# A gated attention and a two-layer net in one hand-ordered program: unit 3's k and q turned by transfers, tiles shared by pairs of units, another order of work

## The chip, the core and the metric

The kernel runs on one core of a Trainium2 chip. A core has five engines that run side by side, each through its own instructions in order: TensorE (PE, matrix products and transposes into the eight PSUM banks), VectorE (DVE), ScalarE (ACT), GpSimd (POOL) and SyncE (SP, which issues the transfers here). Transfers run on 16 DMA engines. An instruction that needs another engine's result waits on a semaphore, and everything behind it on its engine waits too. The metric is the device time of one execution in microseconds (us), lower is better; the median over runs is taken.

## What is computed

```python
def _attn_ref(q, k, v, f_logit):
    f = 1.0 / (1.0 + np.exp(-f_logit))
    state = np.zeros((B, H, D, D))
    for t in range(S):
        state = f[:, :, t, :, None] * state + np.einsum('bhd,bhe->bhde', k[:, :, t], v[:, :, t])
        y[:, :, t] = np.einsum('bhd,bhde->bhe', q[:, :, t], state)

def _moe_ref(x, w_in, w_out):
    h = x @ w_in
    g = np.maximum(0.01 * h, h)
    return g @ w_out

def reference(...):
    x = attn_out.transpose(0, 2, 1, 3).reshape(B * S, H * D)
    return _moe_ref(x, w_in, w_out)
```

B, H, S, D are 4, 8, 768, 48: 4 batches, 8 heads, 768 steps, 48 values a head. So x is 3072 x 384, w_in 384 x 2048 and w_out 2048 x 384. Inputs and output are float32; the kernel multiplies in bfloat16 and adds in float32.

## The kernel before

**Units.** The 768 steps are cut into 6 chunks of 128. The work is staged in 12 units of 256 rows of x. Units 0 to 3 hold one batch each, chunks 0 and 1 ("paired": neighbouring steps share a row of the tile, and a unit's halves are its heads 0 to 3 and 4 to 7). Units 4 to 11 hold two batches each at one chunk from 2 to 5, and their halves are the batches. A state goes on from chunk to chunk, so a unit needs the units of the same batches before it.

**Steps of a unit.** The gates' logits are loaded, and ScalarE makes the softplus of their negative (ge, line 236, and gl, 248). TensorE adds these up over the steps (cs, 257 to 268), ScalarE takes the exponentials (dec, 276 to 285: em for k, at for q, end for the state). VectorE or GpSimd scales k and q by them (line 301). k and q have to be turned, so that the head's values lie along the partitions. That is done in one of two ways: by TensorE (tk, tq: four transposes a half, line 335) with a copy out of PSUM by VectorE or ScalarE (ck, cq, 348 and 350), or by a DMA transpose of the whole unit that SP issues (xk, xq, 355). TensorE multiplies the turned k and q (sc, 371 and 378), VectorE masks the result (mk, 388 and 392), TensorE adds masked scores times v and q times state (mx and ms, 409), and ScalarE or VectorE copies x, already transposed, into the x tile (xt, 469 and 471). The state is updated by pt (482, 487), sf (497, 499) and sb (505, 508).

**The two layers.** A first-layer word (up, 516) is six matmuls of 128 x 256 into one bank; ScalarE applies the leaky relu on the way out (pr, 521) into the g tile. A second-layer word (dn, 528) is four matmuls of 128 x 384. The last half tile goes in two column halves (dh, 550; oh, 557 and 559; sh). ob (572, 574) copies the result into an osb tile and st (578) stores it. Weights are loaded by WI and WO in float32 into staging tiles (`parts_in`, two of 384 KB, and `ring`, three of 768 KB) and cast to bfloat16 by cw (199, 201).

**Fillers.** id_N (207) is N groups of 128 columns of matmul over a tile of ones, whose result nobody reads, four groups to an instruction.

**Order.** One string, `order`, lists all words, some 800 of them, and each word's function is called in that order. Each engine's instructions, and the transfers on SP's queue, come in just this order; nothing reorders them. A word such as `up_2_5@5` is first-layer group 5 of unit 2 into bank 5; a last number of a copy or scaling chooses the engine. The framework adds the waits by which tiles an instruction reads and writes.

**What the change touches.** `lasts` (line 69) and `osbs` (79) have memory of their own. There are three x tiles (77) and three g tiles (78), one unit in each, chosen by `xTs[j % 3]` and `gTs[j % 3]`. Units 0 to 3 turn k and q by TensorE, units 4 to 11 by DMA transposes.

Of the kernel before, what the change touches and what calls it, by code (L numbers as in the profile page):

```python
# [15 lines left out]
def kernel(  # L16
# [442 lines left out]
    def x_out(j, i, e):  # L459
        src = banks[st[j].pop(("py", i))][:, 0:KD]  # L460
        xT = xTs[j % 3]
        if paired(j):
            src = src.rearrange("t (k s n) -> t k s n", k=NK, s=2)
            dst = xT[:, :, i, :].rearrange("t k (n s) -> t k s n", s=2)
        else:
            src = src.rearrange("t (k n) -> t k n", k=NK)
            dst = xT[:, :, i, :]
        if e:
            nc.scalar.copy(out=dst, in_=src)  # L469
        else:  # L470
            nc.vector.tensor_copy(out=dst, in_=src)  # L471
# [37 lines left out]

    def up(j, g, bank):  # L510
        st[j]["pm", g] = bank
        pm = banks[bank].rearrange("t (i n) -> t i n", i=2)
        for i in range(2):
            ff = 2 * g + i
            for kk in range(NK):
                nc.tensor.matmul(pm[:, i, :], w_in_of(ff, kk), xTs[j % 3][:, kk].rearrange("t a s -> t (a s)"),  # L516
                                 start=(kk == 0), stop=(kk == NK - 1))
# [4 lines left out]

    def down(j, a, quarter, *bank):
# [3 lines left out]
        for ff in range(4 * quarter, 4 * quarter + 4):  # L527
            nc.tensor.matmul(po, gTs[j % 3][:, ff, 128 * a:128 * a + 128], w_out_b[quarter][:, ff % 4, :],  # L528
# [164 lines left out]
```

## Time and profile before

| | us |
|---|---|
| median of 3 runs (177.96 to 178.77) | 178.56 |
| the profiled execution | 178.35 |
| its span, from the first to the last recorded event | 176.6 |
| TensorE busy in it | 170.0 |
| ScalarE, VectorE, GpSimd busy | 119.7, 89.3, 55.9 |

The profile page lists each engine's busy time, then the span in 40 slices of 4.4 us (a digit is the busy share of a slice in tenths, PEclk the clock granted to TensorE, DMA the busy share of the transfer engines). A group row names line, engine, operation, out<-in and count, then the busy time, the mean length of one in ns, and the idle time just before, with what ended it. A row in order of time begins with its start and length. An instruction's length includes the time until its result is there; matmuls follow each other closer than that, so their cost is read from start to start.

### The profile page before, as it was taken

The numbers are of one execution on the slowest core, as the hardware profiler recorded it, in microseconds if no ns is written. First come the engines' busy times: TensorE is split into PE (matmuls) and PEld (weight loads), VectorE is DVE, ScalarE is ACT, GpSimd is POOL, SyncE is SP. The second block draws the span as 40 slices with busy tenths as digits, with TensorE's granted clock in tenths as the row PEclk, the third lists the DMA queues.
The fourth block names the chain that finished last, engine by engine and source line by source line (L and its number), as shares of the span: only waits on it lengthen the run. The fifth ranks groups of instructions, "written<-read, shape, count | busy, mean of one in ns | idle before, by whom it ended". The sixth has DMA issues, their size and how long they took to land.

```text
span 176.6 us, 5545 instructions
## 1 busy us (share of the span) xinstructions
PE 170.0 (96%) x2295; PEld 129.7 (73%) x2295; DVE 89.3 (51%) x194; ACT 119.7 (68%) x244; POOL 55.9 (32%) x103
## 2 busy tenths in 40 slices
PE   7998989999899999999999999999999999999992
...
PEclk9999999999999999999999999999999999999999
DMA  5999999999899888789899899999889993300023
GB/s 139 282 301 262 344 341 339 388 296 219 185 198 193 166 182 162 171 214 206 169 203 207 213 182 183 189 242 205 190 170 208 196 222 112 137 4 0 0 71 111
DMA packets 106856, 34.44 MB, mean 195 GB/s; under 512 B 101072, under 2 KB 105040, under 8 KB 106832
## 3 DMA queue, kind: packets, MB, share of 16 engines
...
q8 instruction: 18, 0.29, 0.7%
...
## 4 chain that ended last, share of the span: by engine, by line
PE 71%; SPq 14%; DMA 10%; POOL 1%; issue 1%; DVE 1%; ACT 0%; DVEq 0%
PE ps L516 30%; PE ps L528 29%; SPq L158 9%; PE ps L409 5%; DMA ring<-in_moe_w_in_dram 4%; DMA k_raw<-in_k_dram 3%; DMA ring<-in_moe_w_out_dram 3%; SPq L162 3%; SPq L176 3%; PE ps L378 3%; PE ps L550 2%; PE ps L265 1%; PE ps L487 1%; POOL w_out L201 1%; ACT w_in L199 0%
## 5 line engine op out<-in xcount | busy, mean ns | idle before, releaser
L516 PE MATMUL ps<-xT,w_in 128*128 128x256 bf16 x576 | 70.0, 273 | 0.7 <-ACT w_in L199 0.7
L521 ACT ACTIVATE gT<-ps 128x512 bf16<-128x512 f32 x96 | 55.6, 610 | 21.6 <-PE ps L516 19.3
L528 PE MATMUL ps<-w_out,gT 128*128 128x384 bf16 x368 | 68.4, 326 | 0.0
L516 PEld LDWEIGHTS <-w_in 128*128 128x128 bf16 x576 | 60.8, 110 | 6.2 <-ACT w_in L199 0.9
L528 PEld LDWEIGHTS <-gT 128*128 128x128 bf16 x368 | 34.2, 98 | 19.1
L392 DVE TENSOR_TENSOR wm<-ps,ut 128x512 bf16<-128x512 f32 x32 | 20.1, 684 | 14.0 <-ACT gT L521 8.0
L307 POOL CAST vb<-v_raw 128x768 bf16<-128x768 f32 (+1 forms) x11 | 8.1, 738 | 31.7 <-DMA v_raw<-in_v_dram 29.1
L505 POOL TENSOR_TENSOR sf<-sf,end 128x192 f32<-128x192 f32 x12 | 6.9, 571 | 31.3 <-DVE sf L499 27.5
L301 POOL TENSOR_TENSOR kh<-k_raw,em 128x768 bf16<-128x768 f32 (+1 forms) x8 | 11.7, 1458 | 12.8 <-DMA k_raw<-in_k_dram 6.7
L301 DVE TENSOR_TENSOR qh<-q_raw,at 128x384 bf16<-128x384 f32 (+1 forms) x11 | 9.2, 845 | 11.4 <-DMA q_raw<-in_q_dram 7.8
L574 DVE COPY osb<-ps 128x384 f32<-128x384 f32 x12 | 6.6, 556 | 15.0 <-PE ps L528 13.5
L276 ACT ACTIVATE em<-ps 128x384 bf16<-128x384 f32 x24 | 12.1, 503 | 2.0 <-PE ps L265 1.2
L469 ACT CAST xT<-ps 128x384 bf16<-128x384 f32 x11 | 5.6, 534 | 11.1 <-PE ps L409 11.0
L236 ACT ACTIVATE f_raw<-f_raw 128x384 f32<-128x384 f32 (+1 forms) x16 | 10.8, 689 | 3.1 <-DMA f_raw<-in_f_logit_dram 2.9
L508 POOL CAST sb<-sf 64x192 bf16<-64x192 f32 x30 | 11.3, 376 | 3.6 <-DVE sf L497 1.9
L471 DVE CAST xT<-ps 128x384 bf16<-128x384 f32 x13 | 7.2, 567 | 10.1 <-PE ps L409 10.0
L277 ACT ACTIVATE at<-ps 128x384 bf16<-128x384 f32 x24 | 12.2, 508 | 0.0
L499 DVE TENSOR_TENSOR sf<-sf,ps 64x192 f32<-64x192 f32 x32 | 11.2, 351 | 0.7
L207 PE MATMUL ps<-warm 128*128 128x512 bf16 (+3 forms) x31 | 10.2, 441 | 1.1 <-DVE warm L83 1.1
L388 DVE TENSOR_TENSOR wm<-ps,pair_mask 128x512 bf16<-128x512 f32 x16 | 10.1, 686 | 1.9 <-PE ps L371 1.8
L248 ACT ACTIVATE lf<-f_raw 128x384 bf16<-128x384 f32 (+1 forms) x16 | 10.7, 687 | 0.2
L572 ACT COPY osb<-ps 128x384 f32<-128x384 f32 x11 | 5.3, 479 | 8.1 <-PE ps L528 8.0
...
## 6 DMA issues: line engine op xcount, KB each, us to landing
...
```

Source lines behind the costliest of these rows:

```text
L158: nc.sync.dma_start(out=by_pair(raw(j, x))[:, h].rearrange("t h s d -> t h (s d)"), in_=srcs[x][j, h, 0:2 * C, :].rearrange("h (t s) d -> ...
L236: nc.scalar.activation(gates(j)[:, part], gates(j)[:, part], AF.Exp, scale=-1.0)
L248: nc.scalar.activation(dst, src, AF.Ln, bias=1.0)
L276: nc.scalar.activation(ems[j % 2][:, a], t[:, 0:H * D], AF.Exp, scale=1.0)
L277: nc.scalar.activation(ats[j % 2][:, a], t[:, 0:H * D], AF.Exp, scale=-1.0)
L301: eng.tensor_mul(heads(j, to[j % NR], a)[:, :, :, 0:D], raw_heads(j, x, a), decays(j, by, a))
L392: nc.vector.tensor_mul(w, src.rearrange("t (p n) -> t p n", p=P2), ut[:, None, :].to_broadcast([128, P2, 128]))
L499: nc.vector.tensor_add(sf[rows], sf[rows], new)
L508: eng.tensor_copy(out=sb[rows, :, y * D:y * D + D], in_=sf[rows])
L516: nc.tensor.matmul(pm[:, i, :], w_in_of(ff, kk), xTs[j % 3][:, kk].rearrange("t a s -> t (a s)"), start=(kk == 0), stop=(kk == NK - 1))
L521: nc.scalar.activation(gTs[j % 3][:, 2 * g:2 * g + 2, :], pm, AF.Prelu, alpha=0.01)
L528: nc.tensor.matmul(po, gTs[j % 3][:, ff, 128 * a:128 * a + 128], w_out_b[quarter][:, ff % 4, :], start=(ff == 0), stop=(ff == NF - 1))
```

## The change

It has four parts. x and g tiles hold a pair of units each and there are two of either, so that four units' strips exist where three did; `x_of` and `g_of` pick a unit's strip. `osbs` and `lasts` become views of the staging tiles. Two functions, `up_both` and `relu_both` with the words uq and pq, are added that would do one first-layer product for both units of a pair. The order is new throughout: 785 words instead of 795. In it, unit 3's tk, tq, ck and cq (8 words) are replaced by xk_3 and xq_3; the fillers are 30, 33, 7, 5, 17, 19, 5 and 3 groups instead of 40, 16, 4, 3, 3, 5, 3, 16, 5, 6, 8 and 3; the engines of some copies and scalings are others. TensorE has 2282 matmuls instead of 2295. No word uq or pq stands in the new order. The diff, with the order cut to its start, the stretch around units 2 to 5, and its end:

```diff
@@ -66,7 +66,6 @@
     ems = tiles(2, [128, 2, H * D], BF16, "em")
     ats = tiles(2, [128, 2, H * D], BF16, "at")
     ends = tiles(4, [128, 2, P2], FP32, "end")
-    lasts = tiles(2, [128, 2 * H * D], FP32, "last")
     vbs = tiles(3, [128, 2, H, D], BF16, "vb")
     v2s = tiles(3, [128, 2 * P2, 4, 16], BF16, "v2")
     kTs = tiles(2, [128, 2 * P2, 128], BF16, "kT")
@@ -74,9 +73,8 @@
     wms = tiles(8, [128, 4, 128], BF16, "wm")
     sfs = tiles(B, [128, P2, D], FP32, "sf")
     sbs = [tiles(2, [128, P2, 2 * D], BF16, f"sb{b}_") for b in range(B)]
-    xTs = tiles(3, [128, NK, 2, 128], BF16, "xT")
-    gTs = tiles(3, [128, NF, 256], BF16, "gT")
-    osbs = tiles(4, [128, KD], FP32, "osb")
+    xTs = tiles(2, [128, NK, 2, 2, 128], BF16, "xT")
+    gTs = tiles(2, [128, NF, 2, 256], BF16, "gT")
     banks = [psum.tile([128, 512], FP32, name=f"ps{i}", tag=f"ps{i}") for i in range(8)]
 
     warm = const.tile([128, 128], BF16, tag="warm")
@@ -131,6 +129,9 @@
     NS, SMALL = 3, PIECES.count(256)
     parts_in = tiles(SMALL, [128, NK, 256], FP32, "part")
     ring = tiles(NS, [128, 4 * KD], FP32, "ring")
+
+    osbs = [t.rearrange("p k n -> p (k n)")[:, KD * i:KD * i + KD] for t in parts_in for i in range(2)]
+    lasts = [t[:, 0:2 * H * D] for t in ring[:2]]
 
 
 
@@ -458,7 +459,7 @@
 
     def x_out(j, i, e):
         src = banks[st[j].pop(("py", i))][:, 0:KD]
-        xT = xTs[j % 3]
+        xT = x_of(j)
         if paired(j):
             src = src.rearrange("t (k s n) -> t k s n", k=NK, s=2)
             dst = xT[:, :, i, :].rearrange("t k (n s) -> t k s n", s=2)
@@ -507,25 +508,42 @@
             rows = slice(64 * y, 64 * y + 64)
             eng.tensor_copy(out=sb[rows, :, y * D:y * D + D], in_=sf[rows])
 
+    def x_of(j):
+        return xTs[j // 2 % 2][:, :, j % 2]
+
+    def g_of(j):
+        return gTs[j // 2 % 2][:, :, j % 2]
+
     def up(j, g, bank):
         st[j]["pm", g] = bank
         pm = banks[bank].rearrange("t (i n) -> t i n", i=2)
         for i in range(2):
             ff = 2 * g + i
             for kk in range(NK):
-                nc.tensor.matmul(pm[:, i, :], w_in_of(ff, kk), xTs[j % 3][:, kk].rearrange("t a s -> t (a s)"),
+                nc.tensor.matmul(pm[:, i, :], w_in_of(ff, kk), x_of(j)[:, kk].rearrange("t a s -> t (a s)"),
                                  start=(kk == 0), stop=(kk == NK - 1))
 
     def relu(j, g):
         pm = banks[st[j].pop(("pm", g))].rearrange("t (i n) -> t i n", i=2)
-        nc.scalar.activation(gTs[j % 3][:, 2 * g:2 * g + 2, :], pm, AF.Prelu, alpha=0.01)
+        nc.scalar.activation(g_of(j)[:, 2 * g:2 * g + 2, :], pm, AF.Prelu, alpha=0.01)
+
+    def up_both(j, ff, bank):
+
+        st[j]["pm", ff] = bank
+        for kk in range(NK):
+            nc.tensor.matmul(banks[bank], w_in_of(ff, kk), xTs[j // 2 % 2][:, kk].rearrange("t u a s -> t (u a s)"),
+                             start=(kk == 0), stop=(kk == NK - 1))
+
+    def relu_both(j, ff):
+        nc.scalar.activation(gTs[j // 2 % 2][:, ff].rearrange("t u n -> t (u n)"), banks[st[j].pop(("pm", ff))],
+                             AF.Prelu, alpha=0.01)
 
     def down(j, a, quarter, *bank):
         if bank:
             st[j]["po", a] = bank[0]
         po = banks[st[j]["po", a]][:, 0:KD]
         for ff in range(4 * quarter, 4 * quarter + 4):
-            nc.tensor.matmul(po, gTs[j % 3][:, ff, 128 * a:128 * a + 128], w_out_b[quarter][:, ff % 4, :],
+            nc.tensor.matmul(po, g_of(j)[:, ff, 128 * a:128 * a + 128], w_out_b[quarter][:, ff % 4, :],
                              start=(ff == 0), stop=(ff == NF - 1))
 
     def out_tile(j, a):
@@ -547,7 +565,7 @@
             st[j]["po", a] = bank[0]
         cols = slice(half * KD // 2, half * KD // 2 + KD // 2)
         for ff in range(NF):
-            nc.tensor.matmul(banks[st[j]["po", a]][:, cols], gTs[j % 3][:, ff, 128 * a:128 * a + 128],
+            nc.tensor.matmul(banks[st[j]["po", a]][:, cols], g_of(j)[:, ff, 128 * a:128 * a + 128],
                              w_out_b[ff // 4][:, ff % 4, cols], start=(ff == 0), stop=(ff == NF - 1))
 
     def out_half(j, a, half, e):
@@ -582,7 +600,7 @@
         "tk": turn("k"), "tq": turn("q"), "ck": turn_out("k"), "cq": turn_out("q"),
         "xk": turn_dma("k"), "xq": turn_dma("q"),
         "sc": score, "mk": mask, "mx": mix, "ms": mix_state, "xt": x_out, "pt": state, "sf": state_add, "sb": state_end,
-        "up": up, "pr": relu, "dn": down, "ob": out_copy, "st": store,
+        "up": up, "pr": relu, "uq": up_both, "pq": relu_both, "dn": down, "ob": out_copy, "st": store,
         "Lf": load("f"), "Lk": load("k"), "Lq": load("q"), "Lv": load("v"),
         "WI": load_w_in, "WO": load_w_out, "cw": cast_w, "id": fill,
         "ed": end_dma, "dh": down_half, "oh": out_half, "sh": store_half,
@@ -591,70 +609,69 @@
 
 
     order = """
-    Lf_0_0 Lf_0_1 Lq_0_1 Lk_0_1 Lk_0_0 Lq_0_0 ge_0_0 Lv_0_2 ge_0_1 Lf_1_2 gl_0_1 Lk_1_2 gl_0_0 id_40@6 cs_0_1@0
-    Lq_1_2 cs_0_0@1 WI_1 dec_0_1 Lv_1_2 k_0_1_0 dec_0_0 q_0_1_0 Lf_2_2 id_16@6 tk_0_1@2 k_0_0_0 ck_0_1_1 id_4@6
-    tq_0_1@3 WI_0 q_0_0_0 cq_0_1_1 id_3@6 tk_0_0@4 ck_0_0_0 id_3@0 tq_0_0@5 sc_0_1@6.7 WI_2 v_0_1_0 cq_0_0_1
-    mk_0_1_0 v_0_0_1 id_5@2 sc_0_0@0.1 mk_0_1_1 id_3@4 pt_0_2@2.3 mk_0_0_0 WI_3 ge_1_0 sf_0_0 gl_1_0 mk_0_0_1
-    ge_1_1 sb_0_0_0 id_16@5 cs_1_0@4 WI_4 gl_1_1 dec_1_0 id_5@6 cs_1_1@5 k_1_0_0 mx_0_2@6.7 dec_1_1 tk_1_0@0
-    q_1_0_0 ms_0 xt_0_0_1 ck_1_0_0 q_1_1_1 tq_1_0@2 xt_0_1_1 sf_0_1 cw_0_1_1 k_1_1_1 cq_1_0_0 id_6@4 tq_1_1@1
-    cq_1_1_0 id_8@6 tk_1_1@4 v_1_0_1 v_1_1_0 sc_1_0@5.0 ck_1_1_1 mk_1_0_0 sb_0_1_0 id_3@3 pt_1_2@6.7 ge_2_1
-    mk_1_0_1 sc_1_1@3.2 ge_2_0 up_0_1@1 sf_1_0 gl_2_1 cw_0_0_2 gl_2_0 cs_2_1@4 mk_1_1_1 pr_0_1 cs_2_0@5 sb_1_0_0
-    mk_1_1_0 dec_2_1 up_0_0@0 mx_1_2@6.2 cw_0_2_1 cw_0_3_0 ms_1 sf_1_1 xt_1_0_1 up_0_3@1 WO_0 pr_0_0 xt_1_1_0
...
-    Lv_3_2 tk_2_0@3 cw_1_3_1 cw_1_2_2 dn_1_0_0@4 ck_2_0_0 pr_1_6 sc_2_1@6.7 sc_2_0@2.5 Lk_3_2 ge_3_0 mk_2_1_1
-    dn_0_0_0@3 ge_3_1 mk_2_0_0 gl_3_0 dn_1_0_1 gl_3_1 mk_2_1_0 up_0_7@1 Lk_4_0 cw_1_4_1 cw_1_5_2 mk_2_0_1
-    cs_3_0@7 pr_0_7 dn_0_1_1 dec_3_0 cs_3_1@2 Lf_5_1 cw_1_6_0 dn_0_0_1 dec_3_1 cw_1_7_0 dn_1_1_0@6 dn_0_0_2
-    Lf_5_0 v_2_1_1 v_2_0_0 dn_1_1_1 dn_1_0_2 Lk_4_1 q_3_1_0 q_3_0_1 pt_2_2@5.1 mx_2_2@7.2 sf_2_0 Lv_4_1 dn_1_0_3
-    xt_2_0_1 sb_2_0_1 tq_3_1@5 Lv_4_0 ge_4_2 sf_2_1 tq_3_0@7 dn_1_1_2 cq_3_1_0 sb_2_1_0 gl_4_2 ms_2 cq_3_0_0
-    Lf_6_1 dn_1_1_3 ob_1_0_0 v_3_1_1 xt_2_1_0 dn_0_0_3 ob_1_1_1 Lf_6_0 k_3_1_0 k_3_0_1 v_3_0_1 cs_4_0@1 ob_0_0_0
-    cs_4_1@5 dn_0_1_2 dec_4_0 Lq_4_0 tk_3_1@7 dn_0_1_3 dec_4_1 ck_3_1_0 Lq_4_1 tk_3_0@4 Lq_5_1 ge_5_2 ob_0_1_0
-    up_2_0@2 ck_3_0_0 pt_3_2@6.3 pr_2_0 sc_3_0@1.7 sf_3_0 gl_5_2 Lk_5_0 sc_3_1@5.0 k_4_2_1 up_2_1@4 mk_3_1_0
-    Lk_5_1 up_2_5@2 mk_3_0_1 pr_2_1 sb_3_0_0 up_2_2@6 mk_3_1_1 pr_2_5 Lq_5_0 up_2_4@5 v_4_2_0 mk_3_0_0 pr_2_2
-    xk_4 sf_3_1 up_2_3@7 pr_2_4 dn_2_1_0@4 sb_3_1_1 pr_2_3 pt_4_1@0 ge_6_2 cs_5_1@2 cs_5_0@1 sf_4_1 up_2_7@6
-    gl_6_2 sb_4_1_1 mx_3_2@3.5 q_4_2_1 pr_2_7 pt_4_0@7 xt_3_0_0 cs_6_0@0 dec_5_0 ms_3 sf_4_0 dn_2_0_0@6 xt_3_1_0
...
+    Lf_0_0 Lf_0_1 Lf_1_2 Lq_0_0 Lk_0_0 ge_0_0 Lv_0_2 gl_0_0 id_30@6 cs_0_0@0 dec_0_0 Lk_0_1 ge_0_1 gl_0_1 Lq_0_1
+    id_33@6 cs_0_1@1 q_0_0_1 Lk_1_2 dec_0_1 k_0_0_0 id_7@6 tq_0_0@2 ge_1_1 Lv_1_2 id_5@6 tk_0_0@3 ge_1_0 v_0_1_0
+    ck_0_0_0 Lq_1_2 gl_1_1 gl_1_0 k_0_1_0 Lf_2_2 cq_0_0_1 id_17@6 cs_1_0@4 q_0_1_0 v_0_0_1 cs_1_1@5 sc_0_0@6.7
+    WI_2 dec_1_1 pt_0_2@0.1 mk_0_0_0 tk_0_1@3 tq_0_1@2 k_1_1_0 ck_0_1_1 cq_0_1_0 tk_1_1@5 dec_1_0 sf_0_0 k_1_0_1
+    mk_0_0_1 ck_1_1_1 WI_0 sb_0_0_1 tk_1_0@6 v_1_0_1 sc_0_1@3.2 ck_1_0_0 WI_3 v_1_1_1 mk_0_1_1 q_1_1_1 mk_0_1_0
+    Lq_2_2 q_1_0_1 id_19@4 tq_1_1@0 ge_2_1 mx_0_2@4.5 ge_2_0 cq_1_1_0 gl_2_1 pt_1_2@7.6 xt_0_0_0 ms_0 sf_1_0
+    WI_1 tq_1_0@2 xt_0_1_1 cs_2_1@3 cw_0_2_0 gl_2_0 cq_1_0_1 Lk_2_2 id_5@4 cs_2_0@0 dec_2_1 cw_0_0_2 sc_1_1@4.7
+    sc_1_0@5.2 dec_2_0 mk_1_0_1 sb_1_0_0 up_0_0@3 mk_1_1_1 cw_0_3_2 pr_0_0 mk_1_0_0 up_0_3@2 WI_4 mk_1_1_0
+    up_0_2@0 cw_0_4_1 cw_0_5_2 sf_0_1 Lv_2_2 pr_0_3 id_3@3 up_0_4@7 q_2_0_0 q_2_1_1 pr_0_2 sf_1_1 up_0_5@3 WO_0
+    pr_0_4 mx_1_2@5.4 pr_0_5 cw_0_1_2 tq_2_0@1 xt_1_0_1 ms_1 cq_2_0_0 tq_2_1@2 sb_0_1_0 xt_1_1_1 up_0_1@0
+    cq_2_1_0 WO_1 up_1_5@6 pr_0_1 k_2_0_0 up_1_0@7 k_2_1_0 pr_1_5 sb_1_1_1 up_1_4@3 Lf_3_2 pr_1_0 cw_0_7_2
...
+    ge_3_1 ge_3_0 dn_0_0_0@1 sf_2_1 gl_3_1 WO_3 gl_3_0 dn_0_1_1 mk_2_1_1 sb_2_1_0 v_3_1_1 mk_2_0_1 cs_3_1@4
+    up_1_7@0 dec_3_1 v_3_0_0 Lf_4_1 cs_3_0@3 cw_1_4_0 pr_1_7 dn_0_0_1 dec_3_0 dn_1_1_0@6 cw_1_5_0 dn_1_0_1
+    Lf_4_0 q_3_1_0 dn_1_1_1 q_3_0_0 dn_1_0_2 k_3_0_0 dn_0_0_2 k_3_1_0 dn_0_1_2 xk_3 mx_2_2@2.4 cw_1_6_1 cw_1_7_2
+    pt_3_2@0.3 xt_2_0_0 xq_3 ms_2 sf_3_0 dn_1_1_2 xt_2_1_1 sb_3_0_1 dn_1_0_3 Lf_5_1 ge_4_2 sf_3_1 Lf_5_0
+    dn_0_1_3 ob_1_0_0 Lv_4_0 sb_3_1_0 dn_1_1_3 gl_4_2 ob_0_1_0 up_2_1@2 ob_1_1_1 up_2_6@0 pr_2_1 Lv_4_1 up_2_0@4
+    pr_2_6 cs_4_0@3 Lk_4_1 pr_2_0 sc_3_1@5.7 sc_3_0@6.2 dec_4_0 mk_3_1_1 cs_4_1@0 Lk_4_0 dn_0_0_3 mk_3_1_0
+    dec_4_1 dn_2_1_0@4 Lq_4_1 ob_0_0_0 ge_5_2 dn_2_0_0@7 mk_3_0_1 Lq_4_0 mk_3_0_0 up_2_2@3 gl_5_2 v_4_2_0
+    up_2_3@5 pr_2_2 Lk_5_0 cs_5_1@0 cs_5_0@1 pr_2_3 mx_3_2@2.6 dec_5_1 up_2_4@3 xt_3_0_0 Lk_5_1 ms_3 k_4_2_1
+    up_2_5@5 xt_3_1_0 st_0_1 pr_2_4 up_2_7@2 pr_2_5 Lq_5_1 dn_2_1_1 pr_2_7 q_4_2_0 up_3_0@0 dec_5_0 Lq_5_0
+    pt_4_0@6 dn_2_1_2 sf_4_0 xk_4 up_3_6@3 pr_3_0 k_5_2_1 sb_4_0_1 dn_2_1_3 pr_3_6 st_0_0 dn_2_0_1 ob_2_1_1 xq_4
+    up_3_1@5 dn_2_0_2 pr_3_1 xk_5 up_3_5@2 q_5_2_0 dn_2_0_3 pr_3_5 Lf_6_1 dn_3_0_0@6 Lf_6_0 ob_2_0_1 up_3_3@1
+    xq_5 up_3_7@0 pr_3_3 up_3_2@3 pr_3_7 Lv_5_1 sc_4_2@4.5.2.7 pr_3_2 dn_3_1_0@1 Lv_5_0 mk_4_0_0 up_3_4@0
...
+    pr_11_7 dn_10_1_2 dh_11_1_0@6 dn_11_0_3 oh_11_1_0_0 sh_11_1_0 dn_10_0_2 ob_11_0_0 dn_10_1_3 st_11_0
+    dn_10_0_3 ob_10_1_1 dh_11_1_1 st_10_1 ob_10_0_0 st_10_0 oh_11_1_1_0 sh_11_1_1
```

More of the change, by code (lines that the diff above doesn't have):

```diff
@@ new lines @@
+    sc_5_2@5.7.0.2 Lf_7_0 xt_4_0_1 xt_4_1_0 dn_3_0_2 v_5_2_0 Lk_6_1 mk_5_1_0 Lq_6_0 cs_6_0@3 mk_5_0_0 pt_4_1@4
+    up_4_3@0 dec_6_0 sf_4_1 up_4_0@5 mk_5_0_1 pr_4_3 sb_4_1_0 cs_6_1@4 Lq_6_1 mk_5_1_1 pr_4_0 pt_5_0@3 pt_5_1@0
+    up_4_1@7 dec_6_1 Lk_6_0 dn_3_0_3 pr_4_1 ed_5 up_4_2@2 ge_7_2 ob_3_0_0 mx_5_2@5.4 pr_4_2 Lf_9_1 gl_7_2
+    up_4_7@7 xt_5_1_0 Lq_7_1 xt_5_0_1 q_6_2_0 up_4_4@6 pr_4_7 Lf_9_0 up_4_6@2 pr_4_4 k_6_2_1 Lf_8_0 sf_5_1
+    cs_7_0@4 cs_7_1@5 pr_4_6 dn_3_1_3 sf_5_0 dec_7_1 up_5_5@7 ob_3_1_0 sb_5_0_0 Lf_8_1 up_5_3@6 sb_5_1_1 xq_6
```

77 lines of the change are left out of this document (33 added, 44 removed).

## The prediction

> **What bounds the kernel now.** First the page's head, its slices and its list of queues.
>
> ```profile
> span 176.6 us, 5545 instructions
> ...
> PE 170.0 (96%) x2295; PEld 129.7 (73%) x2295; DVE 89.3 (51%) x194; ACT 119.7 (68%) x244; POOL 55.9 (32%) x103
> ...
> PE   7998989999899999999999999999999999999992
> ...
> PEclk9999999999999999999999999999999999999999
> DMA  5999999999899888789899899999889993300023
> ...
> q8 instruction: 18, 0.29, 0.7%
> ```
>
> TensorE (PE) works 170.0 of 176.6 us. A row that saves matmuls therefore saves time one for one, and a row that makes TensorE wait costs it one for one. The other engines are at 68% or less. The DMA engines are full until late, so a transfer can be late. The windows say how that is spread over the span.
>
> ```profile
> 0.00:23.00 23.00, 20.41 (x373) 12.47 (x374) 17.11 (x56) 18.02 (x44) 9.50 (x34) 1.00 0.93 270
> 23.00:48.00 25.00, 24.35 (x323) 18.97 (x322) 14.75 (x31) 21.24 (x51) 10.56 (x16) 1.00 0.98 293
> 48.00:80.00 32.00, 32.00 (x496) 25.16 (x494) 20.82 (x45) 23.67 (x46) 11.66 (x18) 1.00 0.90 185
> ...
> 146.00:176.60 30.60, 27.20 (x327) 21.51 (x325) 7.36 (x13) 12.77 (x23) 1.17 (x2) 1.00 0.17 60
> ```
>
> The first column after the length is TensorE's busy time. It lacks 2.59 us before 23, 0.65 before 48, nothing before 80 and 3.40 at the end (the last output's copy and store). So the change can save matmuls, 2.6 + 0.65 of waits, or nothing. TensorE's rows in order of time name the waits; the bracket is the idle time before a row and its releaser.
>
> ```profile
> 1.06 4.45 PE L207 MATMUL ps<-warm 128*128 128x512 bf16 x10 [1.06 <-DVE warm L83]
> 5.30 0.37 PE L257 MATMUL ps<-lf,bu 128*128 128x192 bf16 x1
> ...
> 5.92 0.24 PE L257 MATMUL ps<-lf,bu 128*128 128x192 bf16 x1
> ...
> 6.35 1.02 PE L207 MATMUL ps<-warm 128*128 128x512 bf16 x4
> 7.24 0.40 PE L335 MATMUL ps<-ident,kh 128*128 128x128 bf16 x4
> ...
> 8.96 0.42 PE L371 MATMUL ps<-qT,kT 48*64 48x128 bf16 x16
> 9.31 0.45 PE L207 MATMUL ps<-warm 128*128 128x512 bf16 x2
> ...
> 10.33 0.52 PE L482 MATMUL ps<-vb,kh 64*128 64x96 bf16 x16
> 10.78 1.04 PE L207 MATMUL ps<-warm 128*128 128x512 bf16 x4
> ...
> 17.29 0.52 PE L482 MATMUL ps<-vb,kh 64*128 64x96 bf16 x16 [0.33 <-ACT vb L307]
> 18.07 0.42 PE L371 MATMUL ps<-qT,kT 48*64 48x128 bf16 x16 [0.26 <-ACT kT L348]
> ...
> 22.82 7.39 PE L516 MATMUL ps<-xT,w_in 128*128 128x256 bf16 x66 [0.68 <-ACT w_in L199]
> ...
> 47.67 0.40 PE L335 MATMUL ps<-ident,kh 128*128 128x128 bf16 x4 [0.65 <-DVE kh L301]
> 47.90 0.81 PE L528 MATMUL ps<-w_out,gT 128*128 128x384 bf16 x4
> ```
>
> Start to start, ten cold fillers of 512 columns take up to 4.3 us (0.427 each), four warm ones 0.89 (0.222 each), a half unit's sums 0.43 (5.92 to 6.35), a turn by TensorE 0.23 (47.67 to 47.90), a half unit's scores 0.35, a half unit's state 0.45. First-layer matmuls come (7.39 − 0.27)/65 = 0.11 us apart.
>
> **The change part by part.** *Unit 3's turns.* Four words of four transposes leave TensorE: 4 × 0.23 = −0.9. Four copies leave VectorE, which is at 51% and on no wait named above, so 0. The wait of 0.65 at 47.67 was for unit 3's k in such a turn, and goes with it. Two DMA transposes come into SP's queue instead:
>
> ```profile
> 57.64 2.90 SPq L355 DMA_TRANSPOSE kT<-kh  x1
> 60.66 1.23 SPq L355 DMA_TRANSPOSE qT<-qh  x1
> ...
> kT<-kh SPq DMA_TRANSPOSE x8, 3.2
> ```
>
> Each takes 1.23 us to issue (2.90 at worst) and lands 3.2 after. They are issued some 5 us ahead of unit 3's scores, so about 1 us is to spare; if k's scaling is late, the scores pay up to 1.5. SP works in order: a transpose that waits for its scaled k holds the loads behind it (units 4 and 5's gates, values, k and q), which I price among the rivals. Taken at 0.
>
> *Order, start-up.* The three other waits (0.33 + 0.26 + 0.68 = 1.27) stand at places that the new order takes apart: −1.3. Fillers change from 40 cold and 72 warm groups of 128 columns to 30 cold and 89 warm: 10 × 0.427 + 18 × 0.222 = 8.3 against 7.5 × 0.427 + 22.25 × 0.222 = 8.1, −0.2. Against that, units 0 and 1 go through ScalarE in another order, half by half: gates of one half, its decays, gates of the next. Its rows, and those of the scalings and copies, give the waits.
>
> ```profile
> 3.42 1.10 ACT L236 ACTIVATE f_raw<-f_raw 128x384 f32<-128x384 f32 x2 [1.40 <-DMA f_raw<-in_f_logit_dram]
> ...
> 6.09 0.49 ACT L276 ACTIVATE em<-ps 128x384 bf16<-128x384 f32 x1 [0.60 <-PE ps L262]
> ...
> 6.91 0.51 ACT L276 ACTIVATE em<-ps 128x384 bf16<-128x384 f32 x1
> ...
> 9.07 0.59 ACT L348 COPY qT<-ps 128x512 bf16<-128x512 bf16 x1 [0.24 <-PE ps L335]
> ...
> 10.26 0.52 ACT L236 ACTIVATE f_raw<-f_raw 128x384 f32<-128x384 f32 x1
> ```
>
> ```profile
> 14.97 0.92 POOL L301 TENSOR_TENSOR kh<-k_raw,em 128x384 bf16<-128x384 f32 x1
> ```
>
> ```profile
> L471 DVE CAST xT<-ps 128x384 bf16<-128x384 f32 x13 | 7.2, 567 | 10.1 <-PE ps L409 10.0
> ...
> L301 DVE TENSOR_TENSOR kh<-k_raw,em 128x384 bf16<-128x384 f32 x5 | 2.8, 556 | 2.8 <-DMA k_raw<-in_k_dram 1.6 <-ACT em L276 1.1
> ```
>
> A gate pass of a half takes 0.55 (1.10 for two); decays of a half 0.82 (6.09 to 6.91), and begin 0.79 after the sums' first matmul (5.30 to 6.09). Then, as estimates from these:
> - cs_0_0: gates end at 3.42 + 1.1 = 4.5, fillers at 1.06 + 3.2 = 4.3: +0.2.
> - cs_0_1: decays 0_0 from 5.3 to 6.1, gates 0_1 to 7.2; TensorE arrives at 4.5 + 0.43 + 33 groups (1.83) = 6.8, later if some of these are still cold: +0.2.
> - cs_1_0: decays 0_1 from 8.0 to 8.8, four gate passes 0.41 to 0.55 apart (the two spacings above) to about 10.6; TensorE has sums, two turns and 29 groups, 7.2 + 0.43 + 0.46 + 1.61 = 9.7, by which a part of the lateness is already paid: +0.7.
> - tk_1_1 needs the bank that decays 1_1 free. ScalarE comes to them after one q copy and one value (1.19, 9.07 to 10.26), from 11.8 to 12.6 or later; TensorE has 10.5 + 0.86 + 0.35 + 0.45 + 0.46 = 12.6 before: between 0 and 0.8, taken at +0.4.
> - tk_1_0 needs k_1_0, now on GpSimd (0.92) and not VectorE (0.556), after decays 1_0, the next but one on ScalarE: 12.6 + a copy and the first of the decays at about 0.5 each + 0.92 = 14.5, against 13.0 + 0.23: between 0.7 and 1.4, taken at +1.1.
>
> Together +2.6. Behind these waits on TensorE stand unit 0's scores, state mix and the first layer's start, whose own makers run on meanwhile, so I add nothing for them (0 to 0.7 more).
>
> *Pairs in one tile.* The 512-column functions are not called by the new order: first-layer matmuls keep 256 columns and their number, 0. But two units' strips now lie interleaved in one x tile. In the built program the second matmul of up_0_1 waits for unit 1's copy (ScalarE), and that of up_2_5 and of up_2_7 for a copy of unit 3 by VectorE, which itself waits for the end of the first-layer word before. Nothing like that stands inside such a word before.
>
> ```profile
> L516 PE MATMUL ps<-xT,w_in 128*128 128x256 bf16 x576 | 70.0, 273 | 0.7 <-ACT w_in L199 0.7
> ```
>
> The last matmul of the word ends 0.27 after its start, the copy takes 0.57, and the next but one matmul would have come after 0.22, with one in between issued: a gap of about 0.27 + 0.57 − 0.11 = 0.7 at up_2_7, which follows at once. Between up_2_4 and up_2_5 stands unit 3's state mix, and between unit 1's last mix and up_0_1 a turn (0.23), so 0.4 to 0.5 each. Nothing else of the tensor queue can pass them. Sum +1.6, between 0 (should the copies come early) and 2.1. In exchange, four units' tiles are there where three were, which no wait of before asked for: 0.
>
> *The rest.* `osb` and `last` move into staging buffers whose last cast stands in the order ahead of the first write of either; no transfer is added: 0. Engine changes of single copies are off the path. The end is as before, 3.4 us after the last matmul. The count of instructions on TensorE falls by 13, so its fetches stay about 18.
>
> **Sum**: −0.9 − 0.65 − 1.27 − 0.2 + 2.6 + 1.6 = +1.2. The profiled execution took 178.35 us, 1.75 beyond its span; 179.55 by that. The median of the runs shown is 0.2 above it: **179.8 us**.
>
> **The rivals.**
> *The waits are covered (faster).* The first half units run on ScalarE without the second halves in between, so its chain may be shorter than I add up: passes 0.45 apart and not 0.55 make the dozen before decays 1_0 end 1.2 earlier, and the copies into x tiles may find their engines free at once. With start-up at 1.2 and strips at 0.7 the sum is −0.9 − 0.65 − 1.27 − 0.2 + 1.9 = −1.1, 177.5 us. For it: 0.92 on GpSimd has slack if k_1_0 starts early. Against: tk_1_0's chain has five steps without cover.
> *Break-even.* Start-up 1.9 and strips 1.1: 0, 178.6 us.
> *The clock.* After ten fillers in one piece the granted clock is full, at about 5.3 us. The new order leaves TensorE idle at 4.3, before that. If the clock stays low until such a piece is had again, the 33 groups take 8.25 × 0.427 = 3.5 and not 1.83: cs_0_1 is 1.5 later after its wait of 0.2 is used up, and ScalarE's chain with it: +1.5, 181.3 us. For it: every full-speed row stands behind 4.3 us without a gap. Against: 0.2 is a small gap, and no row shows a small gap lowering the clock (18.07 and 22.82 are warm after 0.3 and 0.7). [...]
> *SP's queue (slower).* Two transposes are 2.5 us of issuing, 5.8 at worst, and a wait for scaled k, at a DMA share of 0.90 to 0.98. What comes behind are units 4 and 5's loads and their transposes. Their cover is seen here:
>
> ```profile
> 65.47 0.62 PE L378 MATMUL ps<-qT,kT 48*128 48x128 bf16 x16
> ```
>
> The q transpose issued at 60.66 lands at about 63.9, 1.6 ahead. A shift of 2.5 to 4 would show as a wait of 0.9 to 2.4 before unit 4's or 5's scores: with the sum, 180.7 to 182.2; I take 181.5. Against: turns, loads and words are all put in another order, and unit 4's scores come later too.
>
> **How the numbers follow.** A measurement here can tell about 0.5%, 0.9 us: below 177.7 is faster, above 179.45 slower. Forecast 0.38 (of it 0.29 slower, 0.08 same, 0.01 faster); covered waits 0.22 (nearly all faster); break-even 0.20 (0.17 same); clock 0.08 and SP's queue 0.12 (slower). Faster 0.24, same 0.26, slower 0.50. The range reaches from the covered waits, 177.3, to the queue's upper case, 182.0; the forecast's own is 178.8 to 180.8.
>
> **What would show it.** Right: no turn of unit 3 on TensorE and no wait of 0.65 for kh; idle time of 0.5 to 1.4 before unit 1's sums and turns, released by ScalarE and GpSimd; gaps of 0.3 to 0.7 inside first-layer words released by xT copies; 27 us of TensorE in the last 30 as before. Wrong: start-up idle under 1.5 us in all (covered waits); fillers at 0.427 after 5.5 us (clock); idle before the scores of units 3 to 5, released by a DMA transpose (queue); or a sum of TensorE's busy time that falls by more or less than 1.1.

## The result, and the profile after

The changed kernel takes 180.48 us (median of 4 runs, 180.13 to 181.05) beside 178.31 for the kernel before (4 runs): a ratio of 1.0102, 95% interval 1.006 to 1.0145. It is slower by 2.2 us, inside the range and on the side that was forecast, 0.7 us above the forecast time. Ratios, here and below, compare fast runs alone, those within 1.5% of the fastest run of the same kernel, while medians hold all runs. The profiled execution took 180.50 us, 2.15 more than the one of before.

First the page of the changed kernel.

```profile
span 178.6 us, 5528 instructions
...
PE 169.6 (95%) x2282; PEld 129.8 (73%) x2282; DVE 90.1 (50%) x194; ACT 120.0 (67%) x243; POOL 56.9 (32%) x100
...
q8 instruction: 18, 0.29, 0.6%
```

TensorE is busy for nearly as long as before and idle for 9.0 us instead of 6.6. The windows, with TensorE's busy time after each length, say where.

```profile
0.00:23.00 23.00, 18.07 (x290) 11.54 (x291) 15.48 (x50) 16.31 (x44) 10.20 (x30) 1.00 0.97 279
23.00:48.00 25.00, 24.75 (x395) 19.33 (x394) 18.26 (x40) 18.92 (x39) 11.46 (x23) 1.00 1.01 282
48.00:80.00 32.00, 31.26 (x427) 23.96 (x424) 16.14 (x30) 24.08 (x48) 8.02 (x12) 1.00 0.97 199
...
146.00:178.60 32.60, 29.56 (x342) 22.89 (x340) 7.81 (x15) 12.43 (x22) 0.00 (x0) 1.00 0.18 64
```

4.9 us are missing before 23, where 2.6 were; 0.74 between 48 and 80, where nothing was; 0.25 before 48, where 0.65 was. The end is 0.4 shorter. TensorE's rows in order of time name every wait but the start's and the end's:

```profile
4.65 0.32 PE L258 MATMUL ps<-lf,bu 128*128 128x192 bf16 x1 [0.21 <-ACT lf L249]
...
5.40 2.31 PE L208 MATMUL ps<-warm 128*128 128x512 bf16 x9
7.54 0.25 PE L258 MATMUL ps<-lf,bu 128*128 128x192 bf16 x1
...
10.78 0.24 PE L258 MATMUL ps<-lf,bu 128*128 128x192 bf16 x1 [0.63 <-ACT lf L249]
...
13.38 0.40 PE L336 MATMUL ps<-ident,kh 128*128 128x128 bf16 x4 [0.26 <-DVE kh L302]
14.96 0.40 PE L336 MATMUL ps<-ident,kh 128*128 128x128 bf16 x4 [1.18 <-POOL kh L302]
...
18.61 0.25 PE L410 MATMUL ps<-wm,vb 64*32 64x128 bf16 x8 [1.37 <-DVE wm L389]
...
22.48 2.16 PE L523 MATMUL ps<-xT,w_in 128*128 128x256 bf16 x18 [0.18 <-ACT end L280]
...
28.31 2.67 PE L523 MATMUL ps<-xT,w_in 128*128 128x256 bf16 x23 [0.25 <-ACT xT L470]
...
58.28 0.82 PE L523 MATMUL ps<-xT,w_in 128*128 128x256 bf16 x6 [0.17 <-DVE xT L472]
59.66 0.71 PE L523 MATMUL ps<-xT,w_in 128*128 128x256 bf16 x5 [0.57 <-DVE xT L472]
```

The first four waits are those of sums and turns (cs_0_0, cs_1_0, tk_1_1, tk_1_0), the last three the waits between strips of one x tile (up_0_1, up_2_5, up_2_7). The wait of 1.37 is the mix of unit 0, held by VectorE's masks. VectorE's rows, and below them GpSimd's, show why the masks were late:

```profile
14.34 0.69 DVE L389 TENSOR_TENSOR wm<-ps,pair_mask 128x512 bf16<-128x512 f32 x1
14.95 1.83 DVE L509 CAST sb<-sf 64x192 bf16<-64x192 f32 x2
16.81 0.42 DVE L351 COPY kT<-ps 128x512 bf16<-128x512 bf16 x1
17.27 1.29 DVE L389 TENSOR_TENSOR wm<-ps,pair_mask 128x512 bf16<-128x512 f32 x2
```

```profile
14.87 1.80 POOL L302 TENSOR_TENSOR qh<-q_raw,at 128x384 bf16<-128x384 f32 x2
19.78 0.82 POOL L202 CAST w_in<-part 128x768 bf16<-128x768 f32 x1 [3.12 <-DMA part<-in_moe_w_in_dram]
```

Two casts of the state, 0.95 and 0.86 us, on VectorE, where the median of its 16 such casts is 0.257, just while GpSimd scales q twice. (GpSimd's second row, a cast of weights, comes up below.) The turns of unit 3 by transfer make no wait:

```profile
43.32 1.34 SPq L356 DMA_TRANSPOSE kT<-kh  x1
44.77 1.27 SPq L356 DMA_TRANSPOSE qT<-qh  x1
```

```profile
51.48 0.64 PE L372 MATMUL ps<-qT,kT 48*64 48x128 bf16 x32
```

They land 4.9 and 4.4 us after their issue starts, the second at 49.2 us, 2.3 ahead of the scores that need it.

### The profile page after: what moved, and what is told of

It is laid out like the page before. It is cut to its first block, busy times and chain, and to the rows that moved or that the text cites. A ratio compares the mean times of both kernels' runs of the same rounds, so it can differ in the third digit from the quotient of the medians.

```text
span 178.6 us, 5528 instructions
## 1 busy us (share of the span) xinstructions
PE 169.6 (95%) x2282; PEld 129.8 (73%) x2282; DVE 90.1 (50%) x194; ACT 120.0 (67%) x243; POOL 56.9 (32%) x100
## 4 chain that ended last, share of the span: by engine, by line
PE 87%; ACT 4%; DVE 4%; DMA 2%; issue 1%; ACTq 0%
PE ps L523 36%; PE ps L546 34%; PE ps L410 6%; PE ps L379 2%; PE ps L266 2%; DMA f_raw<-in_f_logit_dram 2%; PE ps L568 1%; PE ps L208 1%; PE ps L488 1%; DVE wm L389 1%; DVE sb L509 1%; ACT lf L249 1%; ACT f_raw L237 1%; PE ps L483 1%; ACT at L278 1%
## 5 line engine op out<-in xcount | busy, mean ns | idle before, releaser
L546 PE MATMUL ps<-w_out,gT 128*128 128x384 bf16 x368 | 66.7, 326 | 0.0
L546 PEld LDWEIGHTS <-gT 128*128 128x128 bf16 x368 | 34.9, 98 | 19.8
L302 POOL TENSOR_TENSOR qh<-q_raw,at 128x768 bf16<-128x768 f32 (+1 forms) x9 | 12.2, 1362 | 17.7 <-DMA q_raw<-in_q_dram 5.8
L590 ACT COPY part<-ps 128x384 f32<-128x384 f32 x12 | 5.8, 479 | 13.8 <-PE ps L546 13.1
L472 DVE CAST xT<-ps 128x384 bf16<-128x384 f32 x12 | 6.7, 569 | 16.0 <-PE ps L410 12.4
L302 POOL TENSOR_TENSOR kh<-k_raw,em 128x768 bf16<-128x768 f32 (+1 forms) x6 | 9.2, 1525 | 12.9 <-ACT em L277 7.8
L506 POOL TENSOR_TENSOR sf<-sf,end 128x192 f32<-128x192 f32 x10 | 5.7, 567 | 20.3 <-DVE sf L500 20.1
L592 DVE COPY part<-ps 128x384 f32<-128x384 f32 x11 | 6.0, 555 | 7.1 <-PE ps L546 7.0
L302 DVE TENSOR_TENSOR kh<-k_raw,em 128x384 bf16<-128x384 f32 (+1 forms) x10 | 7.4, 759 | 4.3 <-ACT em L277 2.3
```

The source lines that it names most:

```text
L302: eng.tensor_mul(heads(j, to[j % NR], a)[:, :, :, 0:D], raw_heads(j, x, a), decays(j, by, a))
L546: nc.tensor.matmul(po, g_of(j)[:, ff, 128 * a:128 * a + 128], w_out_b[quarter][:, ff % 4, :], start=(ff == 0), stop=(ff == NF - 1))
```

## The experiments

Each ratio is to the kernel before, run beside it on the same chip. Where an execution's mean granted clock is given as 0.99, TensorE ran at half clock for some 3 us of it, as those with a profile show (in three of them the granted clock was 0.50 to 0.53 from 16 to 18 us); elsewhere it is 0.997 to 1.0.

| kernel | ratio (95%) | median us |
|---|---|---|
| changed | 1.0102 (1.006 to 1.0145) | 180.48 |
| changed, run again | 1.0131 (1.0108 to 1.0154) | 180.52 |
| four x tiles | 1.0064 (1.0039 to 1.009) | 179.72 |
| state cast on GpSimd | 1.0105 (1.0056 to 1.0153) | 180.33 |
| unit 3 turned by TensorE | 1.0154 (1.0119 to 1.0189) | 181.22 |
| state cast on GpSimd, filled | 1.018 (1.0135 to 1.0226) | 181.38 |
| start-up mended, four x tiles | 1.0011 (0.9978 to 1.0044) | 178.90 |
| start-up mended, pair tiles | 1.0163 (1.0107 to 1.0218) | 181.64 |
| mended, words by arrival of weights | 0.9982 (0.995 to 1.0013) | 178.45 |
| mended, weights first | 1.0092 (1.0057 to 1.0126) | 180.32 |
| before, unit 3's turns by DMA | 1.0198 (1.0139 to 1.0256) | 182.29 |
| the same, gates later | 1.0141 (1.0068 to 1.0215) | 181.30 |
| before, pair tiles and staging views | 1.0114 (1.0024 to 1.0203) | 180.97 |

**The shared strips.**

```diff
-xTs = tiles(2, [128, NK, 2, 2, 128], BF16, "xT")
+xTs = tiles(4, [128, NK, 2, 128], BF16, "xT")
-    return xTs[j // 2 % 2][:, :, j % 2]
+    return xTs[j % 4]
```

> The changed kernel with an x tile of its own for each of four units; the order is the same. Theory (the waits between strips of a shared tile cost what they show): the idle gaps inside first-layer words (0.25 at 28.3, 0.17 at 58.3 and 0.57 at 59.7 us; start to start 0.42 + 0.37 + 0.73 = 1.5) are gone and the time falls by 1.0 to 1.5 us, to 179.0 to 179.5. Rival (a freed gap only turns into the next wait, since the copies of x and what follows come no earlier): the gaps go, others of the same sum appear within 10 us behind them, and the time stays at 180.2 to 180.7.

The three gaps are gone, and the ratio falls by 0.4 to 0.7%, 0.7 to 1.2 us, by which of the two ratios of the changed kernel one takes. The profiled execution had other waits (0.57 and 0.28 us) and a stretch at half clock at its start, so it does not show by itself what the gaps cost. Next, the pair tiles in the order of before; that kernel also has the views of the staging tiles:

> The kernel before, in its own order, with x and g tiles of two units each as in the changed kernel. Theory (a tile shared by two units makes waits between strips that do not overlap): two gaps appear inside the first-layer words that run while unit 1's x is copied, one of 0.3 to 0.4 for ScalarE's copy and one of 0.6 to 0.75 for VectorE's, near 23 and 24.1 us, none near 58 us since that order copies unit 3's x elsewhere; the time rises by 0.6 to 1.2 us, a ratio of 1.003 to 1.007. Rival (the gaps are filled by what waits for weights anyway, which the first layer does at 22.8 us): the gaps show and the ratio stays within 0.998 to 1.002.

Both gaps come where the copies of unit 1's x fall in that order, over 2 us later than expected:

```profile
25.43 0.82 PE L523 MATMUL ps<-xT,w_in 128*128 128x256 bf16 x6 [0.17 <-ACT xT L470]
26.81 7.25 PE L523 MATMUL ps<-xT,w_in 128*128 128x256 bf16 x65 [0.57 <-DVE xT L472]
60.97 0.32 PE L266 MATMUL ps<-lf,ut 128*128 128x384 bf16 x1 [0.50 <-DVE xT L472]
```

The third row is no gap between strips: it is a sum of gates that waits for VectorE's copy out of its bank. The ratio is unclear by its interval, three of the four executions had a clock of 0.99, and the profiled one also waited 1.44 us for a late v at 18.8; the gaps are shown, their price here is not.

**The state cast.** sb_0_0_1 becomes sb_0_0_0.

> The changed kernel with one digit other: the two casts of unit 0's first state (sb_0_0) on GpSimd instead of VectorE, at the same place of the order. In the changed kernel these two took 0.95 and 0.86 us on VectorE, where the median of this cast there is 0.26, while GpSimd scaled unit 1's q (two of 0.9), and the mask behind them on VectorE released the mix of unit 0 after 1.37 us of idle time. Theory (VectorE's cast is held up while GpSimd works, and that holds the mask): the mask starts near 15.8 instead of 17.3 us, the idle time of 1.37 falls below 0.3, and the time falls by 0.9 to 1.4 us, to 179.1 to 179.6. Rival (the mask is late for its scores or another cause): the mask's start moves by less than 0.4 and the time stays within 0.4 of 180.5; a second rival is that unit 1's q, now 0.8 later on GpSimd, takes the place: a new wait of 0.5 to 0.8 before its turn at 16.7, and a gain of 0.5 at most.

Neither the theory nor a rival holds as put: the masks started 1.4 us earlier, at 15.86, and the median did not move. The row of the fillers and the windows with the granted clock (third number from the right) tell where the gain went in the profiled execution.

```profile
15.73 2.21 PE L208 MATMUL ps<-warm 128*128 128x512 bf16 x5
```

```profile
12.00:14.00 2.00, 1.18 (x24) 0.76 (x16) 1.94 (x6) 1.82 (x7) 0.34 (x1) 1.00 1.12 306
14.00:16.00 2.00, 1.38 (x21) 0.88 (x22) 1.26 (x3) 1.89 (x8) 1.86 (x4) 0.65 1.07 326
16.00:18.00 2.00, 2.00 (x8) 0.87 (x7) 1.15 (x2) 1.35 (x3) 1.11 (x2) 0.50 1.01 360
```

After the idle stretch the clock is halved, and the five fillers, 1.20 us in the changed kernel, take most of what the masks gave. In the changed kernel's own profile the clock stayed full over the same time:

```profile
14.00:16.00 2.00, 1.04 (x22) 0.69 (x23) 1.94 (x4) 2.00 (x9) 2.00 (x3) 1.00 0.98 274
16.00:18.00 2.00, 1.24 (x17) 0.62 (x15) 1.94 (x4) 1.58 (x5) 0.66 (x1) 1.00 1.04 329
```

Two executions without profile had the full clock, and took 179.67 and 180.19 us, which hints at a gain of some tenths and does not show one. To tell the clock from a second cause, the idle time was filled.

```diff
-sb_0_0_1 tk_1_0@6
+sb_0_0_0 id_20@6 tk_1_0@6
```

> The changed kernel with unit 0's first state cast on GpSimd, as in the run before it, and 20 groups of filler (1.1 us at the full clock) in front of the turn of unit 1's k (tk_1_0), where TensorE stood idle for 1.18 us. In the run without the filler the mask came 1.4 us earlier, but the granted clock was 0.65 and 0.50 from 14 to 18 us and the five fillers there took 2.0 us and not 1.06, so the mix of unit 0 was reached no earlier than 18.19 us. Theory (idle time around 13 to 15 us lowers the clock, and the lower clock took the gain): with the idle time filled the granted clock stays at 1.00 to 23 us, the mix starts at 16.8 to 17.4 us, and the time falls by 0.6 to 1.3 us below the run without the filler, though TensorE has more to do: a ratio to the kernel before of 1.003 to 1.007. Rival (the clock falls by a phase of its own or for another reason): it falls again and the ratio stays at 1.009 to 1.015.

In this execution the clock stayed at 1.00 and the mix waited for nothing. Yet the time rose, because something else stood next:

```profile
21.95 0.83 PE L523 MATMUL ps<-xT,w_in 128*128 128x256 bf16 x6 [1.52 <-POOL w_in L202]
23.52 1.50 PE L523 MATMUL ps<-xT,w_in 128*128 128x256 bf16 x12 [0.75 <-POOL w_in L202]
```

```profile
21.07 0.82 POOL L202 CAST w_in<-part 128x768 bf16<-128x768 f32 x1 [3.98 <-DMA part<-in_moe_w_in_dram]
```

GpSimd had waited 3.98 us for the weights to land before it cast them. TensorE had reached the first layer at 20.43 us, 1.9 earlier than in the changed kernel, and lost 2.3 us there in two waits. So in this execution the weights' arrival took the place of the wait of 1.37. How far it does so in the changed kernel is not shown: there the same cast began at 19.78 us and ended at 20.6, 1.9 ahead of the first word. (The executions at a clock of 1.0 took 180.8 and 180.9 us, those at 0.99 181.9 and 182.1.) The changed kernel once more:

> The changed kernel once more, on the chip of these runs, to see which start-up waits and which granted clock come back. Theory: the ratio to the kernel before is 1.006 to 1.015 and the same waits stand at unit 1's sums and turns; where the granted clock falls near 14 to 18 us, the mix of unit 0 waits less than 0.3 for its mask, and where it does not, about 1.4. Rival: the wait of 1.37 for the mask comes back together with the lower clock, and the time is 1 us longer than before.

The same waits came back to 0.01 us (0.63, 0.26, 1.18, 1.37). The cast of the first word's weights came later this time:

```profile
20.84 1.01 POOL L202 CAST w_in<-part 128x768 bf16<-128x768 f32 x1 [4.18 <-DMA part<-in_moe_w_in_dram]
```

TensorE reached the first layer at 22.30 us in the first profile. Had it come 1.37 us earlier, at 20.93, it would have waited for this later cast, which ends at 21.85, and not for the one of the first profile; that is an estimate from these rows. Three of the four executions had a mean clock of 0.99 and took 180.44 to 180.62, the fourth, with the profile, 1.0 and 180.58: here half a clock costs nothing. That it only takes the place of a wait is what the profile of the kernel with four x tiles shows, where the clock is 0.50 from 16 to 18 us and the mix waits for nothing.

**The start-up as a whole.**

```diff
-dec_1_1 ... ck_0_1_1 cq_0_1_0 tk_1_1@5 dec_1_0 sf_0_0 k_1_0_1 ... sb_0_0_1 tk_1_0@6
+dec_1_1 ... dec_1_0 ck_0_1_1 cq_0_1_0 tk_1_1@5 sf_0_0 k_1_0_1 ... sb_0_0_0 id_10@6 tk_1_0@6
```

with the four x tiles.

> The changed kernel with four x tiles of one unit each, unit 0's first state cast on GpSimd, unit 1's second decays ahead of a copy of k on ScalarE (so that its k is scaled some 0.65 us earlier), and 10 groups of filler in front of tk_1_0. Theory (the time lost lies in these start-up waits and in the shared strips): tk_1_0 at 14.2 to 14.4 instead of 14.96 us, the mix of unit 0 at 16.1 to 16.9 instead of 18.6, no gap inside first-layer words, and a ratio to the kernel before of 0.990 to 1.000. Rival (the first layer's weights, loaded and cast by about 20.6 us for its first word, bound the start): the mix is early but the first layer starts at 21.5 or later behind casts or loads, and the ratio is 1.001 to 1.005.

The ratio is 1.001, which is the rival's: the loss is gone, but no gain is left. Idle time before the first layer is 0.95 us in four waits of 0.32 or less; then the first layer, though earlier than the rival has it, waits for casts of weights:

```profile
20.78 0.83 PE L523 MATMUL ps<-xT,w_in 128*128 128x256 bf16 x6 [0.71 <-POOL w_in L202]
22.36 1.50 PE L523 MATMUL ps<-xT,w_in 128*128 128x256 bf16 x12 [0.75 <-POOL w_in L202]
```

Only the x tiles were then made pairs again.

> The mended start-up with the two x tiles of a pair of units as in the changed kernel, so that only the four separate x tiles are taken back. Theory (the strips' waits of 0.25 to 0.4, 0.36 and 0.73 us are a cost of their own): they come back at unit 0's and unit 2's first-layer words, and the time is 0.8 to 1.5 us above that of the mended start-up with four tiles, a ratio to the kernel before of 1.005 to 1.010. Rival (most of them is covered): a ratio of 1.000 to 1.004.

The gaps came back (0.25, 0.18 and 0.57). Two executions at full clock took 179.67 and 179.70, beside a median of 178.6 for the eight of the mended start-up with four tiles at that clock: 1.1 us for the strips, or 0.8 when either is set beside the full-clock runs of the kernel before on its own chip. Four executions with a clock of 0.99 took 181.6 to 182.2, so the ratio of 1.0163 mixes two things.

Two attempts at a version that beats both:

> The kernel of the mended start-up, with the first two pieces of w_in loaded ahead of unit 2's gates (they landed at 18.8 and 19.9 us there, and the first-layer words waited 0.71 and 0.75 for their casts), and with unit 2's gates, sums and turns moved behind the first three first-layer words; two fillers (8 groups) fall away. Theory (what bounds the start-up by now is the time at which the first layer's weights land): the first-layer words start at 18.8 to 19.6 instead of 20.8 us, no wait over 0.4 for a weight's cast before them, and the ratio to the kernel before is 0.986 to 0.996. Rival (unit 2's gates, 2 us later, take the place): waits of 1 us or more in all at unit 2's sums, turns or unit 1's mix, and a ratio of 0.998 to 1.006.

The words started at 19.27 us, and the rival took it all and more: mixes, sums and turns of units 1 and 2 then waited, from 21.87 to 31.65 us. With the loads left alone and the words in the order in which their weights arrive (up_0_2 up_0_3 up_0_0, mx_1_2 ahead of up_0_4):

> The kernel of the mended start-up (ratio 1.001), with unit 0's first-layer words 2 and 3, whose weights land at 18.8 us, ahead of word 0, whose weights land at 19.9, the casts in that order on GpSimd and VectorE, unit 1's mix ahead of word 4, and one filler of 3 groups less. Theory (what is left at the start is TensorE waiting for weights while it has other work): the waits of 0.71 and 0.75 us for GpSimd's casts shrink to under 0.4 in all, and the ratio to the kernel before is 0.991 to 0.998. Rival (the next piece of weights, landing at about 22 us, or unit 2's q at 23.7, takes the place): a wait of 0.6 to 1.0 at word 4 or at unit 2's turns, and a ratio of 0.999 to 1.004.

```profile
21.40 2.13 PE L523 MATMUL ps<-xT,w_in 128*128 128x256 bf16 x18 [1.00 <-ACT end L280]
```

The waits for weights go; one of 1.00 appears in front of the first word, behind ScalarE's decays, which hold its bank. The ratio of 0.998 is 1.2% under that of the changed kernel and cannot be told from the kernel before.

**The turns by DMA.** In the changed kernel, xk_3 and xq_3 gave way to tq_3, tk_3 and VectorE's copies:

> The changed kernel with unit 3's k and q turned by TensorE again and copied by VectorE, in place of the two DMA transposes. Theory (the transposes by DMA take 0.9 us off TensorE and cost nothing else): the time rises by 0.7 to 1.3 us, to 181.2 to 181.8, with no new wait but the turns' own, and the loads on SP's queue behind 50 us land up to 2.5 us earlier without a gain. Rival (two transposes on SP's queue delay loads that the path needs): the time rises by less than 0.4, or falls.

The ratio rises by 0.2 to 0.5%, 0.4 to 0.9 us; TensorE has 32 transposes of either kind again instead of 24. It agrees with the 0.9 us of work that the turns take; the rival (less than 0.4) is not excluded by much. In the order of before:

```diff
-Lf_4_1 ... Lf_4_0 ... Lk_3_2 ... Lf_5_1 ... Lf_5_0 ... Lk_4_1 q_3_1_0 q_3_0_1 ... tq_3_1@5 ... tk_3_0@4
+Lk_3_2 ... Lf_4_1 ... Lf_4_0 ... q_3_1_0 q_3_0_1 xq_3 k_3_0_1 ... k_3_1_0 xk_3 Lf_5_1 Lf_5_0 Lk_4_1
```

> The kernel before with unit 3's k and q turned by DMA transposes, its k loaded right behind its q, and unit 5's gates and half of unit 4's k loaded behind the transposes. Theory: 16 transposes (0.9 us) and the wait of 0.65 for the scaled k at 47.7 us go, the scores of unit 3 wait for nothing, and the time falls by 1.2 to 1.8 us from 178.3, to 176.5 to 177.1. Rival (the transposes land after the scores are reached, or hold loads behind them on SP's queue): an idle gap of 0.5 to 2 us at unit 3's scores or at unit 4's or 5's sums, and a time of 177.8 to 179.5.

```profile
23.15 0.30 PE L409 MATMUL ps<-wm,v 64*32 64x128 bf16 x8 [2.01 <-issue]
53.05 2.78 PE L516 MATMUL ps<-xT,w_in 128*128 128x256 bf16 x24 [2.50 <-ACT gT L521]
57.04 0.33 PE L487 MATMUL ps<-vb,kh 128*128 128x96 bf16 x4 [0.55 <-POOL vb L307]
```

```profile
51.67 0.84 ACT L236 ACTIVATE f_raw<-f_raw 128x768 f32<-128x768 f32 x1 [2.92 <-DMA f_raw<-in_f_logit_dram]
52.42 0.58 ACT L521 ACTIVATE gT<-ps 128x512 bf16<-128x512 f32 x1
```

The rival of SP's queue is seen at work in the row of 53.05 and in ScalarE's: unit 5's gates land late behind the transposes, ScalarE waits for them in order, and the relus behind it stop TensorE. Then the gates went later:

> The kernel before with unit 3's turns by DMA as tried first, but with unit 5's gates three first-layer words later in ScalarE's order, so that their load, held up behind the transposes, no longer stops the relus of unit 2 (a gap of 2.5 us at 53.05 us in the first try). Theory (the turns themselves are worth about 1.5 us here, and only what stands behind them on SP's queue took it back): the gap of 2.5 is under 0.5 and the ratio to the kernel before is 0.990 to 0.998. Rival (the transposes only move the lateness to other loads): gaps of 1 us or more in all before unit 4's and unit 5's states or sums, and a ratio of 1.000 to 1.010.

The gap of 2.5 was gone, but unit 4's values now came late instead (an idle time of 3.51 us at 58.62 in the profiled execution, which took 184.24 us; the others took 179.53 to 181.88). At neither of the two places tried in that order were the transposes free.

## Why the prediction was right, point by point

- *Turns and their wait.* The 16 transposes and the wait of 0.65 are gone, and the scores of unit 3 wait for nothing. Right; the spare time is 2.3 us (44.77 + 4.4 to 51.48), not 1, and they took 4.9 and 4.4 to land, not 3.2. SP's queue made no wait here, but it did at both places tried in the order of before, so what the transposes cost hangs on the order around them.
- *Waits by place.* Forecast 0.2, 0.2, 0.7, 0.4 and 1.1; idle 0.21, none, 0.63, 0.26 and 1.18: 2.3 for 2.6.
- *What stands behind them.* "I add nothing for them (0 to 0.7 more)" was mis-sized, and is the step that failed: the mix of unit 0 waited 1.37 more, and the first word 0.18. The makers did not "run on meanwhile": VectorE's two casts took 1.83 us in all while GpSimd scaled, and the masks came behind them (1.4 us earlier once the casts had gone to GpSimd). The two took 0.95 and 0.86 against a median of 0.257 us, and each ends 0.1 us after one of GpSimd's scalings does. The same stands once more in that profile: casts of 1.67 and 0.79 us from 133.06 on, which end 0.1 us after GpSimd's scaling of k (1.65 us from 132.97) and its cast behind that. Not every overlap does it: from 30.78 and 85.62 us on, four casts beside GpSimd's casts took 0.25 to 0.38. No run here takes the scaling away and leaves the casts, but in the profile of the kernel with four x tiles GpSimd stood idle for 0.88 us ahead of its two scalings, which began at 15.48, and the masks behind the same casts started at 15.66. So that GpSimd's work held the casts up fits these rows; what in the two engines does it is not shown.
- *Strips.* Three gaps at the three words named. Start to start they are 0.42, 0.37 and 0.73 us above the usual spacing, 1.5 for a forecast of 1.6; the experiments price them at 0.7 to 1.2. That the interleaving makes them, and not a shared tile of any layout, no run here separates.
- *The sum.* It took the waits that go as idle time (0.33 + 0.26 + 0.68 + 0.65) and priced the strips from start to start, which is longer by the tail of the last matmul: 1.5 where the idle time is 0.99. That tail counts as busy, and is a part of why TensorE's busy time fell by 0.3 and not 1.1, which the prediction had named as a sign of error; the rest is not worked out. By the windows the span grew by 2.0: idle time +2.34 before 23 us, −0.40 from there to 48, +0.74 to 80, −0.36 at the end, and busy time −0.32. The start-up was forecast at +1.33 (2.6 − 1.27). That the total came within 0.7 us has some luck in it: the end was 0.4 shorter than taken, against 1.55 left out behind the start-up waits.
- *Rivals.* The waits were not covered; they stood as added up. But a limit close behind them was not named, the landing of w_in: GpSimd could cast the first word's piece only at 19.78 us (20.84 in the second profile), and the kernels with a mended start-up waited for that cast. The clock was not lost at 4.3 us: the fillers from 5.40 on are at full speed after the first two (0.38 and 0.41 us from start to start, then 0.216; the granted clock reads 1.00 from 0 us on in both profiles, so a cold stretch shows in the spacing alone). But the sums from 4.65 to 5.40 took 0.75 us and not 0.43, and the 33 groups behind them 2.14 (5.40 to 7.54) and not 1.83, which covers the wait of 0.2 forecast for cs_0_1. The clock is lost later in some executions, near 15 us (0.62 to 0.78 granted between 14 and 16 us in three profiles).

Taken together, strips of about 1 us and a start-up of about 1 us make the 2.2 us; each is shown by the kernels that take it back (1.0064 with four x tiles, 1.0011 with the start-up mended as well). How the start-up's share divides between single waits stays open, since each wait hides another.
